# Two MLPs behind a recurrent attention: 512 tokens at a time, transposed results, and other costs in the loop that orders the work

## The chip, the cores and the metric

The kernel runs on one core of one Trainium2 chip. The metric is the device time of one execution in microseconds; the median of 3 runs counts. The engines are TensorE (PE), VectorE (DVE), ScalarE (ACT), GpSimd (POOL) and SyncE (SP), which issues most of the DMAs.

## The reference

A linear recurrence with complex decay per head (4 batches, 8 heads, 768 tokens, head size 48), then two MLPs over the 3072 tokens of 384 features:

```
a_re_n, a_im_n = a * min(|a|, 0.999) / (|a| + 1e-6)
for t in range(S):
    S_re, S_im = ar*S_re - ai*S_im + k[t] v[t]^T, ar*S_im + ai*S_re
    y[t] = q[t] @ S_re
x = y as (3072, 384)
x = relu(x @ w_in)**2 @ w_out                       # 384 -> 2048 -> 384
xn = x / sqrt(mean(x*x) + 1e-6) * rms_g
out = (silu(xn @ w_gate) * (xn @ w_val)) @ w_out2   # 384 -> 1536 -> 384
```

## The kernel before

The work is cut into 24 **units** of 128 tokens of one batch. Attention makes them two by two: a `chain` on VectorE and ScalarE normalizes the decay and multiplies it up along the tokens (`norm`, `step`, `plevel`), and for each unit PE does transposes (`dtr`, tile dps), scores (`score`, tile sps), results (`yy`, tile yps) and a state update (`state`, tile ups). `fix` moves slices of the result by six small DMAs, and `split_x` splits it into two parts for exact products in a fast float type (tile xs). With the last xs of a group its MLP can begin.

The **first MLP** takes two units at a time (`GROUPS`, L38; 256 tokens). For each of its 16 blocks f of 128 hidden features, `mlp_h` (L799) does nine matmuls with 256 columns into PSUM tile h, ScalarE makes relu and two squares of it (r, gs, h), VectorE a difference (gs), and `mlp_x` (L824) adds the block to the results x by six matmuls, with a part of gs as the stationary operand and 384 columns of weights as the moving one: a result has tokens in its partitions. `store_x` (L837) copies it out, and it goes to a DRAM tile xnd.

The **second MLP** takes three units at a time (`G2`, L938; 384 tokens). `load_x` (L941) fetches them from xnd, `rms` (L949) sums the squares of each token along its row on ScalarE, `turn` (L971) transposes them on PE (tile t), and for each of 12 blocks `mlp_g`, `mlp_v` and `mlp_o` (L998 to L1031) do nine matmuls of 384 columns each. 34 tiles of weights come as 64-bit floats; `convert` (L742) turns each into two parts with passes over ScalarE and VectorE. 18 of them belong to the second MLP, and 16 of these are loaded into the places of the first MLP's tiles as that MLP lets go of them.

The order of all this is made at build time. Each piece of work is a generator that yields an `Op` with its engine, a cost in us, buffers that it takes and gives back, and a priority; `Plan.run` (L98) holds a clock for each engine, and takes again and again the operation that can start first, by priority among those that can start at the same time. `ready` (L83) says when one can start: at the end of what it needs, plus `SYNC` and `PE_END` if that was on another engine. The instructions are issued in that order on each engine; the costs decide nothing else.

```
SYNC, PE_END, LAND = 0.13, 0.1, 2.2
LATE = {"pe": 2.0}
def dve(n): return 0.075 + 0.00104 * n
def act(n): return 0.1 + 0.00083 * n
```

Of the kernel before, what the change touches and what calls it, by code (L numbers as in the profile page):

```python
# [44 lines left out]
def dve2(n):  # L45

    return 0.11 + 0.00116 * n


def act(n):  # L50
    return 0.1 + 0.00083 * n
# [10 lines left out]
class Plan:  # L62
# [20 lines left out]
    def ready(self, j):  # L83

        t, op = j[4], j[3]
        for n in (*j[5], *op.need):
            end, eng = self.t[n]
            t = max(t, end if eng == op.eng else end + SYNC + PE_END * (eng == "pe"))
        for r in op.acq:
            k = self.taken[r] - self.counts[r]  # L90
            if k >= 0:
                if k >= len(self.back[r]):
                    return None
                end, eng = self.back[r][k]
                t = max(t, end if eng == op.eng else end + SYNC + PE_END * (eng == "pe"))
        return t

    def run(self):  # L98
        live = list(self.jobs)
        while live:  # L100
# [14 lines left out]
            for c in best.values():  # L115
                s0 = min(x[0] for x in c)
                now = [x for x in c if x[0] <= s0 + 0.02]
                old = [x for x in now if x[4] <= s0]
# [24 lines left out]
            elif j[3].free:  # L143
                j[4] = max(j[4], s)
            else:
                j[4] = end if j[3].eng == op.eng else end + SYNC + PE_END * (op.eng == "pe")


class Attention:
# [101 lines left out]
    def sumsq(self, m, s, ab, view=lambda t: t, **more):  # L251
# [5 lines left out]
        yield Op("dve", dve2(768))  # L257
# [4 lines left out]
    def norm(self, p):  # L262
# [15 lines left out]
        yield Op("dve", dve2(768))  # L278
        nc.vector.tensor_tensor(out=m, in0=m, in1=r, op=ALU.mult)
        yield Op("dve", dve2(768))  # L280
# [3 lines left out]
        yield Op("dve", dve2(768))  # L284
        nc.vector.scalar_tensor_tensor(out=m, in0=y, scalar=-2.0 / 0.999, in1=r, op0=ALU.max, op1=ALU.mult)
        d = m.rearrange("p (u j d) -> p j u d", u=2, j=8)
        for c, x in enumerate(self.raw.pop(p)):
            yield Op("dve", dve2(768), rel=["raw"] + ["tmp"] * c)
# [5 lines left out]
    def step(self, p, j):  # L294
# [3 lines left out]
        yield Op("dve", dve2(384))  # L298
# [5 lines left out]
        yield Op("dve", dve2(96))  # L304
        nc.vector.tensor_tensor(out=v[:, 0], in0=T[:, 0, 0], in1=T[:, 1, 1], op=ALU.subtract)
        yield Op("dve", dve2(96))
# [16 lines left out]
    def plevel(self, l):  # L323
# [5 lines left out]
        for t, c in ((X, 0), (Y, 1)):  # L329
# [6 lines left out]
            else:  # L336
                for e in range(2):
                    yield Op("dve", 0.2)
# [5 lines left out]
            yield Op("dve", 0.27)  # L344
            nc.vector.tensor_tensor(out=o, in0=i0, in1=i1, op=ALU.mult)
        yield Op("dve", 0.24)
        nc.vector.tensor_tensor(out=V[:, 0, :, s:], in0=X[:, 0], in1=Y[:, 1], op=ALU.subtract)
        yield Op("dve", 0.24, done=("TP", self.at) if l == 3 else None)
        nc.vector.tensor_tensor(out=V[:, 1, :, s:], in0=X[:, 1], in1=Y[:, 0], op=ALU.add)

    def chain(self, p):
# [23 lines left out]
        for n, (o, i0, i1) in enumerate(((x, a[1], f[1]), (y, a[0], f[1]), (a[0], a[0], f[0]), (a[1], a[1], f[0]))):  # L375
            yield Op("dve", dve2(768), rel=["tb"] if n == 3 else [])
            nc.vector.tensor_tensor(out=o, in0=i0, in1=i1, op=ALU.mult)
        yield Op("dve", dve2(768))
        nc.vector.tensor_tensor(out=a[0], in0=a[0], in1=x, op=ALU.subtract)
        yield Op("dve", dve2(768), rel=["tmp", "tmp"], done=("P", p))  # L380
# [19 lines left out]
    def inv(self, p):  # L400
# [13 lines left out]
        yield Op("dve", dve2(768), need=[("kin", p)])  # L414
        k = self.kin[p].rearrange("p u j d -> p (u j d)")
        nc.vector.tensor_tensor(out=m, in0=m, in1=z, op=ALU.mult)
        yield Op("dve", dve2(768))
        nc.vector.tensor_tensor(out=k, in0=k, in1=z, op=ALU.mult)
        yield Op("dve", dve2(768), rel=["tmp", "tmp"], done=("inv", p))
        nc.vector.scalar_tensor_tensor(out=k, in0=m, scalar=2.0, in1=k, op0=ALU.subtract, op1=ALU.mult)  # L420

    def prod(self, u, which):
        p, i = u // 2, u % 2
        o, t = (self.QP, self.qin[p]) if which == "q" else (self.KP[i], self.kin[p])
        for c in range(2):
            rel = [which + "in"] if (i and c) else []
            yield Op("dve", dve(384), acq=[] if c else [which + "P"], rel=rel, done=(which + "P", u) if c else None)
# [133 lines left out]
def general_path(tc, q, k, v, a_re, a_im, w, ident, gcol, out):  # L561
# [3 lines left out]
    with ExitStack() as ctx:  # L565
# [63 lines left out]
        with ExitStack() as c2:  # L629
# [33 lines left out]
            with tc.For_i(0, NT // 128, 1) as it:  # L663
# [22 lines left out]
                acc = ps.tile([128, DM], F32, tag="gacc", name="g_acc2")  # L686
                for f in range(F2):
# [5 lines left out]
                    nc.tensor.matmul(acc, lhsT=g, rhs=words(T_OUT2 + f // 2, f % 2), start=(f == 0), stop=(f == F2 - 1))  # L693
                o = sb.tile([128, DM], F32, tag="go", name="g_o")
                nc.vector.tensor_copy(o, acc)
                nc.sync.dma_start(out[bass.ds(it * 128, 128), :], o)
# [3 lines left out]
def kernel_body(ctx: ExitStack, tc, q, k, v, vt, a_re, a_im, w, rms_g, out):  # L700
# [8 lines left out]
    xnd = dram.tile([NT, DM], F32, name="xnd")  # L709
# [4 lines left out]
    psh = p1.enter_context(tc.tile_pool(name="psh", bufs=3, space=PSUM))  # L714
# [9 lines left out]
        sY=2, pe=4, xt=1, xs=2, h=3, xg=1, r=2, gs=3, x1=2, cr=2, cr2=4, xr=2, gv=3, ys=2, og=1, t=2, uu=2, us=3, ot=3,  # L724
# [17 lines left out]
    def convert(n, on_pe):  # L742

        cr, bufs = ("cr", 2) if on_pe else ("cr2", 4)
# [28 lines left out]
    def do_y(u, g, i):  # L773
        def xt():
            if i == 0:
                n = len(GROUPS[g]) * CH
                xt_t[g] = sb.tile([128, 4, n], F32, tag="xt", name="xt", bufs=1)
                xs_t[g] = sb.tile([128, 2, KT, n], F32R, tag="xs", name="xs", bufs=2)
            return xt_t[g][:, :, i * CH:(i + 1) * CH]

        if i == 0:
            yield Op("none", 0, acq=["xt", "xs"])
        yield from att.yy(u, xt)

    def fix(u, g, i):
        xt, sl = xt_t[g], slice(i * CH, (i + 1) * CH)
# [5 lines left out]
    def split_x(u, g, i):  # L792
        sl = slice(i * CH, (i + 1) * CH)
        xs = xs_t[g]
        yield from split(
            xs[:, 0, :, sl], xs[:, 1, :, sl], xt_t[g][:, 0:KT, sl], DM, rel=["xt"] if i else [], done=("xs", u)
        )

    def mlp_h(g, f):  # L799
        n = len(GROUPS[g]) * CH  # L800
        yield Op("pe", 1.06, acq=["h"], rel=["xs"] if f == F1 - 1 else [], done=("h", g, f), p=MLP_PE)
# [10 lines left out]
        yield Op("act", act(256), acq=["r"])  # L812
        r = sb.tile([128, n], F32, tag="r", name="r", bufs=2)
        nc.scalar.activation(out=r, in_=hp, func=AF.Relu)  # L814
        yield Op("act", act(256), acq=["gs"])
        gs = sb.tile([128, 2, n], F32R, tag="gs", name="gs", bufs=3)
        nc.scalar.activation(out=gs[:, 0], in_=r, func=AF.Square)  # L817
        yield Op("act", act(256), rel=["r"])
        nc.scalar.activation(out=hp, in_=r, func=AF.Square)  # L819
        yield Op("dve", dve(256), rel=["h"], done=("gs", g, f))  # L820
# [3 lines left out]
    def mlp_x(g, f):  # L824
        nb = len(GROUPS[g])
        yield Op("pe", 1.06, acq=[] if f else ["xg"], rel=["gs"], done=("x", g, f), p=MLP_PE)
        if f == 0:
            x_ps[g] = [psx.tile([128, DM], F32, tag=f"x{i}", name=f"x{i}") for i in range(nb)]
        gs = g_t.pop((g, f))
        for i in range(nb):  # L830
# [6 lines left out]
    def store_x(g, i, u):  # L837
        if i == 0:
# [289 lines left out]
```

## Time and profile before

| | |
|---|---|
| runs (us) | 1145.86, 1147.71, 1148.03 |
| median | 1147.71 us |
| profiled execution, its own time from first to last instruction (the span) | 1147.8 us |
| PE busy | 1084.5 us (94%) |
| VectorE busy | 720.2 us (63%) |
| ScalarE busy | 628.3 us (55%) |
| GpSimd busy | 100.6 us (9%) |

The profile is one execution. A share over the whole span mixes three stages: a start in which weights are converted while the first units are made, a long middle in which attention and the first MLP run together, and the second MLP alone. What a change is worth is read stage by stage. Matmuls are pipelined and their ends are modelled, so the distance from one start to the next tells PE's pace better than its busy time.

### The profile page before, as it was taken

The page shows a single profiled execution, that of the slowest core. Times are in us where ns is not written, and L with a number is a line of the kernel's source. Part 1 is how long each engine was busy: PE and PEld are TensorE (multiplying, and loading weights), DVE is VectorE, ACT ScalarE, POOL GpSimd, SP SyncE. Part 2 cuts the span into 40 slices and gives each one's busy share as a digit, 9 for nine tenths or more (in the row PEclk, how much of TensorE's full clock was granted, in tenths as well). Part 3 has the DMA queues.
Part 4 walks back from the last instruction along what each step waited for, and adds up shares of the span by engine and source line. Part 5 has one row for each costly group of instructions (what it writes and reads, how often), then busy time and mean ns, then how long its engine had stood idle before and what let it go on. Part 6 is the DMA issues. An engine that isn't in the chain of part 4 may idle for free.

```text
span 1147.8 us, 20154 instructions
## 1 busy us (share of the span) xinstructions
PE 1084.5 (94%) x7876; PEld 1039.6 (91%) x7876; DVE 720.2 (63%) x1468; ACT 628.3 (55%) x1387; POOL 100.6 (9%) x90
## 2 busy tenths in 40 slices
PE   1679889999999999999999999999999999999997
PEld 0468679999999999999999988999999999999997
DVE  5999999998989988998622579632323232222221
ACT  3878866668577766665655899432323232222221
POOL 0011123022121221220000000000000000000000
PEclk9799999999999999999999999999999999999999
DMA  8733141423514423331001780010101000000000
GB/s 276 302 87 103 33 127 47 121 55 107 143 40 121 113 68 102 87 88 38 23 11 40 253 331 2 9 33 10 33 11 32 11 32 11 12 11 11 13 9 24
DMA packets 79063, 85.41 MB, mean 74 GB/s; under 512 B 47728, under 2 KB 74608, under 8 KB 78960
## 3 DMA queue, kind: packets, MB, share of 16 engines
q1 hardware_dynamic: 78824, 83.85, 23.8%
q8 instruction: 64, 1.05, 0.4%
q14 instruction: 39, 0.32, 0.1%
q10 hardware_dynamic: 136, 0.20, 0.1%
HBM read 64.23 MB, written 18.61 MB: 72 GB/s over the span
## 4 chain that ended last, share of the span: by engine, by line
PE 83%; DVE 6%; ACT 5%; DMA 3%; issue 1%; SPq 1%; DVEq 0%; ACTq 0%
PE h L807 17%; PE x L832 17%; PE v L992 12%; PE o L1028 12%; PE g L992 12%; PE sps L467 3%; PE dps L454 3%; DMA ws<-in_w 3%; PE yps L484 2%; PE ups L502 2%; PE yps L488 2%; ACT ws L535 1%; DVE ws L537 1%; DVE cr L541 1%; ACT cr L533 1%
## 5 line engine op out<-in xcount | busy, mean ns | idle before, releaser
L807 PE MATMUL h<-xs,w 128*128 128x256 f32 x1728 | 242.2, 285 | 3.0 <-ACT w L761 1.8
L832 PE MATMUL x<-w,gs 128*128 128x384 f32 x1152 | 241.3, 344 | 2.3 <-ACT gs L817 1.3
L807 PEld LDWEIGHTS h<-xs,w 128*128 128x128 f32 x1728 | 224.8, 189 | 7.0 <-ACT w L761 2.4
L832 PEld LDWEIGHTS x<-w,gs 128*128 128x128 f32 x1152 | 194.1, 190 | 6.8 <-DVE gs L821 2.2
L1014 DVE TENSOR_TENSOR uu<-t,v 128x384 f32<-128x384 f32 x96 | 53.1, 554 | 195.8 <-PE v L992 194.5
L1028 PE MATMUL o<-w,us 128*128 128x384 f32 x864 | 166.9, 336 | 2.9 <-ACT us L729 2.5
L992 PE MATMUL g<-ys,w 128*128 128x384 f32 x864 | 167.0, 337 | 1.3 <-DVE w L731 0.5
L992 PE MATMUL v<-ys,w 128*128 128x384 f32 x864 | 167.4, 338 | 0.0
L1028 PEld LDWEIGHTS o<-w,us 128*128 128x128 f32 x864 | 151.0, 188 | 5.1 <-ACT us L729 3.1
L992 PEld LDWEIGHTS g<-ys,w 128*128 128x128 f32 x864 | 151.7, 188 | 2.7 <-DVE w L731 1.4
L992 PEld LDWEIGHTS v<-ys,w 128*128 128x128 f32 x864 | 150.3, 188 | 0.1
L814 ACT ACTIVATE r<-h 128x256 f32<-128x256 f32 x192 | 72.9, 380 | 122.9 <-PE h L807 122.4
L1005 ACT ACTIVATE t<-g 128x384 f32<-128x384 f32 x96 | 47.3, 493 | 159.9 <-PE g L992 159.8
L729 ACT CAST us<-uu 128x384 fp32r<-128x384 f32 x96 | 49.2, 513 | 131.2 <-DVE uu L1014 131.2
L821 DVE TENSOR_TENSOR gs<-h,gs 128x256 fp32r<-128x256 f32 x192 | 80.4, 419 | 58.8 <-ACT h L819 57.9
L731 DVE TENSOR_TENSOR us<-uu,us 128x384 fp32r<-128x384 f32 x96 | 53.6, 558 | 50.2 <-ACT us L729 50.2
L817 ACT ACTIVATE gs<-r 128x256 fp32r<-128x256 f32 x192 | 80.3, 418 | 8.7 <-PE x L832 2.7
L512 POOL TENSOR_TENSOR Y<-W,pe 48x384 f32<-48x384 f32 x40 | 52.1, 1302 | 320.3 <-DVE W L508 174.6
L819 ACT ACTIVATE h<-r 128x256 f32<-128x256 f32 x192 | 71.2, 371 | 0.0
L467 PE MATMUL sps<-dq,dk 112*128 112x128 f32 x384 | 52.6, 282 | 4.3 <-ACT dq L456 1.8
L467 PEld LDWEIGHTS sps<-dq,dk 112*128 112x128 f32 x384 | 49.3, 197 | 6.2 <-ACT dq L456 2.7
L300 DVE TENSOR_TENSOR XY<-A 128x384 f32<-128x384 f32 x84 | 49.0, 583 | 2.2
(123 smaller groups left out, 1338.7 us busy)
## 6 DMA issues: line engine op xcount, KB each, us to landing
ws<-in_w SPq DMA_DIRECT2D x34, 768.0 KB
kb<-KP SPq DMA_DIRECT2D x20, 448.0 KB
kt<-kb SPq DMA_DIRECT2D x20, 448.0 KB
raw<-in_a_re SPq DMA_DIRECT2D x24, 192.0 KB
raw<-in_a_im SPq DMA_DIRECT2D x24, 192.0 KB
kin<-in_k SPq DMA_DIRECT2D x24, 192.0 KB
qin<-in_q SPq DMA_DIRECT2D x24, 192.0 KB
V<-in_vt SPq DMA_DIRECT2D x24, 192.0 KB
```

The lines of the kernel that those rows point to most:

```text
L467: nc.tensor.matmul(P[:, i], lhsT=K[:, h, :], rhs=Q[:, h, :], start=True, stop=True)
L512: nc.gpsimd.tensor_tensor(out=Y[dst:dst + D], in0=W[src:src + D], in1=im[src:src + D].to_broadcast([D, H, D]), op=ALU.mult)
L731: nc.vector.tensor_tensor(out=lo, in0=src, in1=hi.bitcast(F32), op=ALU.subtract)
L807: nc.tensor.matmul(hp, lhsT=part(f, 0, a)[:, kk * 128:(kk + 1) * 128], rhs=xs[:, bb, kk, :], start=(i == 0), stop=(i == 8),)
L814: nc.scalar.activation(out=r, in_=hp, func=AF.Relu)
L817: nc.scalar.activation(out=gs[:, 0], in_=r, func=AF.Square)
L819: nc.scalar.activation(out=hp, in_=r, func=AF.Square)
L821: nc.vector.tensor_tensor(out=gs[:, 1], in0=hp, in1=gs[:, 0].bitcast(F32), op=ALU.subtract)
L832: nc.tensor.matmul(x_ps[g][i], lhsT=gs[:, a, i * CH:(i + 1) * CH], rhs=part(f, 1, bb), start=(f == 0 and n == 0), stop=(f == F1 - 1 and n ...
L992: nc.tensor.matmul(P, lhsT=part(T_GATE + f, half, a)[:, kk * 128:(kk + 1) * 128], rhs=ys[:, bb, kk, :], start=(i == 0), stop=(i == 8),)
L1014: nc.vector.tensor_tensor(out=uu, in0=t_t.pop((g, f)), in1=P, op=ALU.mult)
L1028: nc.tensor.matmul(o_ps[g][i], lhsT=us[:, a, i * CH:(i + 1) * CH], rhs=part(T_OUT2 + f // 2, f % 2, bb), start=(f == 0 and n == 0), stop=( ...
```

## The change

- The first MLP takes its first four units two by two as before, then four units (512 tokens) at a time; the second MLP takes four units at a time.
- `mlp_x` and `mlp_o` swap their operands: 128 columns of weights are the stationary operand, and gs (us) with all tokens of the group the moving one. Results have features in their partitions; xnd and the output are transposed, and the host turns the output back.
- The sum of squares now runs along partitions: two matmuls with a matrix of ones (tile rsum) replace the transposes t, and the normalization works on whole tiles of 128 x 512 and 128 x 1536.
- Buffers: h 3 to 2, gs 3 to 2, one xr and one ys for each of two pools.
- The loop that orders the work has other costs, adds a time after an operation for the next one that needs it also on the same engine (not on PE), marks independent neighbours as `free` (they may start with the one before), and may wait up to 0.3 us for an operation of very high priority.

The diff, cut to its core:

```diff
-SYNC, PE_END, LAND = 0.13, 0.1, 2.2
+LAND = 2.2
+AFTER = {"pe": 0.2, "dve": 0.115, "act": 0.095, "pool": 0.12}
+URGENT, NEAR = -250, 0.3
 LATE = {"pe": 2.0}
-GROUPS = [[2 * i, 2 * i + 1] for i in range(12)]
+GROUPS = [[0, 1], [2, 3]] + [list(range(u, u + 4)) for u in range(4, 24, 4)]
+def mm(k, n):
+    return k * (0.006 + 0.0004375 * n)
 def dve(n):
-    return 0.075 + 0.00104 * n
+    return 0.067 + n / 960
 def act(n):
-    return 0.1 + 0.00083 * n
+    return 0.097 + n / 1200
+def after(of, to):
+    return 0.0 if of == to == "pe" else AFTER.get(of, 0.0)
...
-                t = max(t, end if eng == op.eng else end + SYNC + PE_END * (eng == "pe"))
+                t = max(t, end + after(eng, op.eng))
...
+                now += [x for x in c if s0 + 0.02 < x[0] <= s0 + NEAR and x[1] <= URGENT]
-                old = [x for x in now if x[4] <= s0]
+                old = [x for x in now if x[4] <= max(s0, x[0])]
...
+    def turned_out(ps, w, src, first, last):
+        for e in range(KT):
             for n, (a, bb) in enumerate(PASS):
                 nc.tensor.matmul(
-                    x_ps[g][i], lhsT=gs[:, a, i * CH:(i + 1) * CH], rhs=part(f, 1, bb),
-                    start=(f == 0 and n == 0), stop=(f == F1 - 1 and n == 2),
+                    ps[e], lhsT=w(bb)[:, e * 128:(e + 1) * 128], rhs=src[:, a, :],
+                    start=(first and n == 0), stop=(last and n == 2),
                 )
...
+            need = [("xs", u) for u in us] + [("w", f, 0), ("w", f if g == 0 else F1 - 1, 1)]
...
-    G2 = [[3 * i, 3 * i + 1, 3 * i + 2] for i in range(8)]
+    G2 = [[4 * i + j for j in range(4)] for i in range(6)]
...
+        yield Op("pe", mm(2, N2), acq=["gv"])
+        P = P2["psg"].tile([128, N2], F32, tag="gv", name="rsum")
+        for i in range(2):
+            nc.tensor.matmul(P, lhsT=ones, rhs=hl[:, i], start=(i == 0), stop=(i == 1))
```

The change makes another order of nearly all instructions. Three places of it follow.

The first place is PE between the second pair of units (group 1) and the next group of the first MLP. Before, with x_1674 and x_1675 the results of group 1 and x_2281, x_2282 those of group 2:

```order
L807 MATMUL h<-xs,w 128x256 x9
L454 MATMUL dps<-ident,KP_90 112x128 x4
L832 MATMUL x_1674<-w,gs 128x384 x3
L832 MATMUL x_1675<-w,gs 128x384 x3
L807 MATMUL h<-xs,w 128x256 x18
L832 MATMUL x_2281<-w,gs 128x384 x3
L832 MATMUL x_2282<-w,gs 128x384 x3
```

Now, where the first h of 512 columns stands (yps of the eighth unit ahead of it, dps and sps belong to the ninth):

```order
L491 MATMUL yps<-st,V_90 64x128 x2
L495 MATMUL yps<-dq,St_102 48x128 x2
L461 MATMUL dps<-ident,QP 112x128 x8
L461 MATMUL dps<-ident,KP_91 112x128 x8
L826 MATMUL h<-xs,w 128x512 x9
L474 MATMUL sps<-dq,dk 128x128 x4
```

Before, h of the next pair stands among the last blocks of the pair before it; now the last x of group 1 stands 56 rows ahead of the first h of the quad, and between them are only attention's instructions, those of the seventh and the eighth unit.

The second place is VectorE in the attention chain, some way before the eighth unit is ready (A is the decay, XY a product of two of its steps, kin the keys). Before:

```order
L821 TENSOR_TENSOR gs<-h,gs 128x256
L300 TENSOR_TENSOR XY<-A_86 128x384
L305 TENSOR_TENSOR A_86<-XY 128x96
L307 TENSOR_TENSOR A_86<-XY 128x96
L300 TENSOR_TENSOR XY<-A_86 128x384
L821 TENSOR_TENSOR gs<-h,gs 128x256
```

Now:

```order
L425 TENSOR_TENSOR kin<-kin,z 128x768
L840 TENSOR_TENSOR gs<-h,gs 128x256
L427 SCALAR_TENSOR_TENSOR kin<-m,kin 128x768
L312 TENSOR_TENSOR A_87<-XY 128x96
L435 TENSOR_TENSOR KP_91<-A_88,kin 128x8x48 x2
L314 TENSOR_TENSOR A_87<-XY 128x96
```

Before, an A reads the XY just before it and the next XY the A just before it; now a row of other work stands between an instruction and the one that reads it.

The third place is ScalarE around the change from the first to the second MLP. Before, around the first silu (t) of the second MLP (cr, ws and w are the passes of a conversion):

```order
L729 CAST w<-cr 128x768
L551 ACT_TABLE_LOAD
L551 ACTIVATE rs_y<-ss 128x3
L533 ACTIVATE cr<-ws 128x768
L535 ACTIVATE ws<-ws 128x768
L533 ACTIVATE cr<-ws 128x768
L729 CAST us<-uu 128x384
L1005 ACT_TABLE_LOAD
L1005 ACTIVATE t<-g 128x384
```

Now, one step f of the last quad of the first MLP:

```order
L540 ACTIVATE cr<-ws 128x768
L833 ACTIVATE r<-h 128x512
L745 CAST w<-cr 128x768
L542 ACTIVATE ws<-ws 128x768
L836 ACTIVATE gs<-r 128x512
L838 ACTIVATE h<-r 128x512
```

Before, the first silu has six of the 18 conversions' last pass (w) ahead of it; now each step of the last quad holds one conversion, and 16 stand ahead of the first silu.

## Rows read from the trace of the kernel before

**Rows 1.** The page: span, busy us with share and instructions by engine, PE's 40 slices.
```profile
span 1147.8 us, 20154 instructions
...
PE 1084.5 (94%) x7876; PEld 1039.6 (91%) x7876; DVE 720.2 (63%) x1468; ACT 628.3 (55%) x1387; POOL 100.6 (9%) x90
...
PE   1679889999999999999999999999999999999997
```

**Rows 2.** Timeline, PE, second MLP: start us, us, engine line op names shapes xcount.
```profile
900.43 1.73 PE L992 MATMUL g<-ys,w 128*128 128x384 f32 x9
...
905.12 1.72 PE L992 MATMUL g<-ys,w 128*128 128x384 f32 x9
...
911.37 0.49 PE L978 MATMUL t<-ident,xr 128*128 128x128 f32 x3
911.62 0.59 PE L992 MATMUL v<-ys,w 128*128 128x384 f32 x2
```

**Rows 3.** Timeline, PE, first MLP behind the last attention block.
```profile
620.76 1.34 PE L807 MATMUL h<-xs,w 128*128 128x256 f32 x9
621.94 1.21 PE L832 MATMUL x<-w,gs 128*128 128x384 f32 x6
622.99 1.23 PE L807 MATMUL h<-xs,w 128*128 128x256 f32 x9
624.06 1.21 PE L832 MATMUL x<-w,gs 128*128 128x384 f32 x6
```

**Rows 4.** Windows: stretch, us, PE PEld DVE ACT POOL busy (x), PEclk, DMA share, GB/s.
```profile
164.10:202.20 38.10, 38.02 (x364) 36.92 (x365) 35.23 (x80) 26.28 (x65) 9.98 (x8) 1.00 0.29 78
202.20:260.40 58.20, 57.88 (x512) 56.04 (x511) 54.72 (x122) 39.03 (x97) 11.04 (x8) 1.00 0.35 95
260.40:305.00 44.60, 44.60 (x415) 43.23 (x413) 40.65 (x87) 30.26 (x75) 9.65 (x8) 1.00 0.37 100
305.00:351.40 46.40, 46.40 (x428) 44.76 (x427) 41.46 (x88) 31.92 (x79) 9.52 (x8) 1.00 0.34 93
```

**Rows 5.** Timeline, DVE, around the xs of the 12th unit.
```profile
350.00 0.56 DVE L300 TENSOR_TENSOR XY<-A 128x384 f32<-128x384 f32 x1
350.48 0.42 DVE L821 TENSOR_TENSOR gs<-h,gs 128x256 fp32r<-128x256 f32 x1
350.81 0.55 DVE L731 TENSOR_TENSOR xs<-xt,xs 128x384 fp32r<-128x384 f32 x1
```

**Rows 6.** Timeline, PE, first h of the sixth pair.
```profile
356.34 1.23 PE L807 MATMUL h<-xs,w 128*128 128x256 f32 x9
```

**Rows 7.** Lines by form, DVE: xcount | busy us, mean ns | idle before us.
```profile
L377 DVE TENSOR_TENSOR x<-A,back 128x768 f32<-128x768 f32 x24 | 22.0, 946 | 2.3 <-PE back L365 2.2
```

**Rows 8.** Timeline, DVE, a step of the attention chain.
```profile
300.63 0.56 DVE L300 TENSOR_TENSOR XY<-A 128x384 f32<-128x384 f32 x1
301.23 0.26 DVE L305 TENSOR_TENSOR A<-XY 128x96 f32<-128x96 f32 x1
```

**Rows 9.** Timeline, PE, the longest wait after the first MLP.
```profile
684.72 1.55 PE L1028 MATMUL o<-w,us 128*128 128x384 f32 x6 [1.51 <-ACT us L729]
```

**Rows 10.** Lines by form, ScalarE (ACT).
```profile
L814 ACT ACTIVATE r<-h 128x256 f32<-128x256 f32 x192 | 72.9, 380 | 122.9 <-PE h L807 122.4
...
L1005 ACT ACTIVATE t<-g 128x384 f32<-128x384 f32 x96 | 47.3, 493 | 159.9 <-PE g L992 159.8
L535 ACT ACTIVATE ws<-ws 128x768 int32<-128x768 uint8 x34 | 31.3, 920 | 0.0
...
L729 ACT CAST w<-cr 128x768 fp32r<-128x768 f32 x18 | 15.1, 841 | 2.8 <-DVE cr L541 2.8
```

**Rows 11.** Timeline, all engines, the end.
```profile
1140.16 0.48 ACT L1040 COPY ot<-o 128x384 f32<-128x384 f32 x1 [0.57 <-PE o L1028]
1140.67 1.21 ACTq L1043 DMA_DIRECT2D out<-ot  x1
```

**Rows 12.** Windows, the second MLP, columns as in rows 4.
```profile
800.00:900.00 100.00, 100.00 (x582) 99.82 (x581) 31.11 (x65) 33.60 (x69) 0.00 (x0) 1.00 0.08 25
```

More of the change, by code (lines that the diff above doesn't have):

```diff
@@ L145, in run @@
             else:
[L146 removed]
+                j[4] = end + after(op.eng, j[3].eng)
 class Attention:
@@ new lines, in turned_out, with mlp_x, store_x @@
+                    start=(first and n == 0), stop=(last and n == 2),
+                )
+    def mlp_x(g, f):
+        n = len(GROUPS[g]) * CH
+        yield Op("pe", mm(9, n), acq=[] if f else ["xg"], rel=["gs"], done=("x", g, f), p=MLP_PE)
+        if f == 0:
+            x_ps[g] = [psx.tile([128, n], F32, tag=f"x{e}", name=f"x{e}") for e in range(KT)]
+        turned_out(x_ps[g], lambda bb: part(f, 1, bb), g_t.pop((g, f)), f == 0, f == F1 - 1)
+    def store_x(g, e):
+        n = len(GROUPS[g]) * CH
+        yield Op("dve" if e == 1 else "act", dve(n), acq=["r"], done=("xc", g, e))
+        x = sb.tile([128, n], F32, tag="r", name="x1", bufs=2)
+        if e == 1:
+            nc.vector.tensor_copy(x, x_ps[g][e])
+        else:
+            nc.scalar.copy(out=x, in_=x_ps[g][e])
+        yield Op("sp", 0.65, rel=["r"], mb=0.27, done=("xnd", g, e))
+        nc.sync.dma_start(xnd[e * 128:(e + 1) * 128, GROUPS[g][0] * CH:GROUPS[g][0] * CH + n], x)
@@ L1023, in mlp_o @@
         if f == 0:
-            o_ps[g] = [P2["pso"].tile([128, DM], F32, tag=f"o{i}", name=f"o{i}") for i in range(nb)]
-        us = u_t.pop((g, f))
-        for i in range(nb):
-            for n, (a, bb) in enumerate(PASS):
-                nc.tensor.matmul(
-                    o_ps[g][i], lhsT=us[:, a, i * CH:(i + 1) * CH], rhs=part(T_OUT2 + f // 2, f % 2, bb),
-                    start=(f == 0 and n == 0), stop=(f == F2 - 1 and n == 2),
-                )
-    def store(g, i):
-        b, c = att.bc(G2[g][i])
-        yield Op("dve" if i == 1 else "act", dve(DM), acq=["ot"], done=("oc", g, i))
-        t = P2["sb"].tile([128, DM], F32, tag="ot", name="ot", bufs=3)
-        if i == 1:
-            nc.vector.tensor_copy(t, o_ps[g][i])
-        else:
-            nc.scalar.copy(out=t, in_=o_ps[g][i])
-        end = (g, i) == (len(G2) - 1, 2)
-        yield Op("act" if end else "sp", 0.65, mb=0.2, rel=["ot"])
-        (nc.scalar if end else nc.sync).dma_start(
-            out[b * S_LEN + c * CH:b * S_LEN + (c + 1) * CH, :].rearrange("(p j) e -> j p e", j=8), t
-        )
+            o_ps[g] = [P2["pso"].tile([128, N2], F32, tag=f"o{e}", name=f"o{e}") for e in range(KT)]
@@ new lines, in mlp_o, with store @@
+        turned_out(o_ps[g], lambda bb: part(T_OUT2 + f // 2, f % 2, bb), u_t.pop((g, f)), f == 0, f == F2 - 1)
+    def store(g, e):
+        yield Op("dve" if e == 1 else "act", dve(N2), acq=["ot"], done=("oc", g, e))
+        t = P2["late"].tile([128, N2], F32, tag="ot", name="ot", bufs=3)
+        if e == 1:
+            nc.vector.tensor_copy(t, o_ps[g][e])
+        else:
+            nc.scalar.copy(out=t, in_=o_ps[g][e])
+        end = (g, e) == (len(G2) - 1, 2)
+        yield Op("act" if end else "sp", 0.65, mb=0.27, rel=["ot"])
+        dst = out[e * 128:(e + 1) * 128].rearrange("e (b c t) -> e b c t", b=B, c=NC)[:, :, g, :]
+        (nc.scalar if end else nc.sync).dma_start(dst, t.rearrange("e (b t) -> e b t", b=B))
@@ L1065, in kernel_body @@
             plan.job(s + LAG2 + 0.2, mlp_o(g, f), ["open3", ("us", g, f), ("w", T_OUT2 + f // 2)] + before)
[L1066 to L1068 removed]
+        for e in range(KT):
+            plan.job(t0 + F2, store(g, e), [("o", g, F2 - 1)])
+        plan.job(t0, join([("oc", g, e) for e in range(KT)], ["og"]))
     order = []
@@ L1081, in kernel_body @@
         nc.scalar.mul(minus, ident, -1.0)
+        nc.scalar.activation(out=ones, in_=ident, func=AF.Copy, scale=0.0, bias=1.0)
         nc.sync.dma_start(gcol, rms_g.rearrange("(k p) -> p k", p=128))
```

277 lines of the change are left out of this document (133 added, 144 removed).

## The prediction, made before the changed kernel ran

> **What bounds the kernel now.** I read the page first [rows 1]: TensorE (PE) is busy for 1084.5 of 1147.8 us, and the digits of the 40 slices stand at 9 from the seventh on. The ends of matmuls are modelled, so I then read their spacing in the timeline. In the second MLP [rows 2] g starts at 900.43 and the next g at 905.12: 27 matmuls of 384 columns in 4.69 us, 173.7 ns each, back to back. In the first MLP [rows 3] nine h matmuls of 256 columns take 1.07 us (119 ns each) behind an MLP block, and six x matmuls of 384 take 1.05; the h that follows an attention block (yps) takes 1.18, so a switch from attention back to an MLP costs about 0.1. Wherever PE has work it runs at its rate; the end is PE's work plus the time in which it had none.
>
> The second view is the table of windows, whose bounds I set where a group's last xs is ready: the 4th, 6th, 8th, 10th and 12th unit of 128 tokens [rows 4]. PE is full in all four, but VectorE (DVE) is busy for 35.23 + 54.72 + 40.65 + 41.46 = 172.1 of 187.3 us. So while attention runs there are two bounds, and units arrive at VectorE's pace. The 12th xs ends at 351.36 [rows 5], and h of the sixth pair starts at 356.34 [rows 6].
>
> **The change, part by part.** I work out when h of the first quad that needs the 12th unit's successors can start, that is the quad of units 8 to 11, and add what is then left. The sum is made on the profiled span of 1147.8 us, 0.1 above the median of the runs.
>
> *The pair that comes later.* A group of four units can start only when its fourth is ready. Before, the pairs of units 4, 5 and 6, 7 ran while the next were made; now, by the order, PE has after group 1 only attention until the eighth unit is ready (first place above). When units 8 to 11 are ready, PE has therefore done four pairs' worth where before it had done five (the sixth started at 356.34). A pair is 16 x (1.07 + 1.05) = 33.9 us [rows 3]. PE's idle time in between cannot be won back, since PE is the bound in all that follows.
>
> *When the 12th unit is ready.* Both orders put almost the same number of VectorE instructions before it, 653 and 650. Counted by kind: gs of 256 goes from 78 to 32, with 16 of 512 beside them. A gs is followed after 0.33 us (350.48 to 350.81), a 384-wide product after 0.48 (350.00 to 350.48) [rows 5], so 512 is 0.62 [estimate]: 25.7 against 20.5 us, -5.2. Copies of x: -0.6. In their place the new order holds some 27 more of the attention chain, five of 768 (0.946) [rows 7] and the others small, like the 0.26 at 301.23: +9.2 with their overlap taken off. Neighbours where one reads what the one before writes go from 176 to 136; such a pair costs 0.12 (300.63 to 301.23 is 0.60 against the 0.48) [rows 8]: -4.8. Together -1.4. Of VectorE's 15.2 us idle in rows 4 I take 3 as gone, because PE stands ready for attention in the empty stretch; the bounds are 0 and 11. So the 12th xs ends at 351.4 - 1.4 - 3 = 347.0, and h starts 1.4 later, at **348.4** (bounds 338 and 352). The lower bound is PE's: the eighth unit has 443 instructions before it where it had 480, and 48 dependent neighbours fewer, about 18 us in all, so it comes at 242.4; from there 16 x 4.12 for the quad and 28 for attention with its switches (before: 356.3 - 260.4 = 96 less two pairs of 33.9) give 242.4 + 1.4 + 94 = 338.
>
> *What is left from there.* Before, 1147.8 - 356.3 = 791.5 us.
> - One pair more: +33.9. Two x blocks of the group before, still to do at 356.3 and done by now: -2.1.
> - Wider matmuls. From 256 to 384 columns the spacing grows by 55 ns; the same step again gives 229 ns for 512 [estimate]. A quad is 16 x 2 x 9 x 0.229 = 66.0 against 67.8 for two pairs: four quads, -7.4. The second MLP: 96 x 4.69 = 450.2 against 72 x 27 x 0.229 = 445.2, -5.0. Bounds of the one unknown: 227.0 (128 more columns at 2.4 GHz, 53.3 ns) and 231.6 (in proportion to 384), on 3,096 such matmuls from there on and 288 before: -7 and +9.
> - The transposes: 24 blocks of 0.25 us (911.37 to 911.62) [rows 2] go, six rsum of two 512-column matmuls (0.46) come: -3.3. With 18 switches fewer: -1.8.
> - Switches between attention and MLP from there on, counted in the order: 77 become 61, -1.6.
> - From the first to the second MLP. PE waited for us behind weight conversions on ScalarE, 1.51 us the longest [rows 9]; five such waits stand in the timeline, 4.0 us. In the order (third place above) six of the 18 tiles were converted when ScalarE came to its first silu; now it is 16. I take -3.0; bounds -4 and +4. The cost is that each step of the last quad now holds three 512-wide activations and one conversion. By the rows 256 takes 0.380 and 384 takes 0.493 [rows 10], so 512 about 0.61; 3 x 0.61 and a conversion's three passes of 0.92, the same again and 0.84 would be 4.5 us against PE's 4.12, but activations that follow each other overlap by nearly 0.1, six times, which brings it to 3.9.
> - The tail: last copy at 1140.16, last store at 1140.67 [rows 11]. The copy is a third wider and the store goes out in rows of 128 tokens instead of 384 features: +0.7, bounds 0 and +1.5.
> - Nothing: SyncE issues fewer transfers (stores of x 24 to 21, loads of it 24 to 6, outputs 24 to 18), the larger rms work on ScalarE and VectorE lies beside a second MLP that leaves both about 67% idle [rows 12] (cover gone: about 5 us for a group), and two buffers of h and gs instead of three have 2 us of slack a step (a rival, below).
>
> That is 791.5 + 33.9 - 2.1 - 7.4 - 5.0 - 3.3 - 1.8 - 1.6 - 3.0 + 0.7 = 801.9, and **348.4 + 801.9 = 1150.3 us**. The wider matmuls and the smoother order give back nearly all of the late pair, and no more.
>
> The Trainium skill (TensorE: Matmul & The Clock Gate, Back-to-back issue gap) gives the spacing of an isolated warm matmul as its columns at 2.4 GHz plus 2.5 ns, 162.5 ns at 384 and 215.8 at 512. With 215.8 for 229 the sum would be some 45 us lower; but the trace has 173.7 where the rule has 162.5, in a stream with a weight load before each matmul, so the measurement decides. Of the rule only the price of a further column remains open, and that is the second rival below.
>
> **The rivals.** *VectorE stops waiting* (faster). The order now prices dependent steps and so fills the gaps; if its idle time in rows 4 falls from 15.2 to about 7, PE decides and the quad starts at 340: 1142. For it: the new order puts other work between dependent steps (second place above). Against it: the four stretches are already 92% busy, and the empty stretch has fewer gs to fill gaps with. It decides below some 8 us of idle between the 4th and the 12th unit. *A matmul has a fixed part* (faster): if further columns cost just 2.4 GHz, 512 takes 227.0 ns, and 3,384 of them give 1143.5. Two sizes cannot exclude it, but 119 and 173.7 lie on a line with 55, not 53.3. *Two buffers* (slower): ScalarE cannot square step f+2 before x of step f has freed gs; from there two squares, the subtraction and their hand-overs take 2.0 us, and PE wants the h buffer 4.1 us later. One 768-wide activation and one 768-wide product in the way use that up; 0.1 us in each of 80 steps is 8 us: 1158. *The order's own times are short* (slower): it prices a 768-wide product at 0.867 us where the row has 0.946 [rows 7]. If that 9% is real on the 172 us of rows 4, PE waits in its fixed order where the plan thinks all is ready, and some 10 us of it come on top: 1160. Against it: an independent neighbour follows a 384-wide product after 0.48, close to the 0.467 of the plan.
>
> **How the numbers follow.** The forecast gets 0.43, with 1146 to 1155 of its own from the bounds of the start of the quad and of the tail; VectorE stops waiting 0.27; the fixed part 0.08; the two slower ones 0.22 together. Over 0.2% (about what a measurement here can tell) means below 1145.4 or above 1150.0. The forecast lies on the upper edge: about 0.20 of its chance is the same, 0.23 slower. So faster 0.28 (0.22 + 0.06), same 0.27, slower 0.45. The range of 8 in 10 reaches from the two faster cases to the two slower ones: 1140 to 1161.
>
> **What would show it.** Right: in the windows of the new profile PE is clearly below full between about 200 and 243 us; VectorE stays above 90% until the 12th xs near 347; h of the fourth group starts at 346 to 350; h of 512 steps in 2.06; the waits of o for us are gone; PE is full from 350 to the end. Wrong: the quad starts before 342 or after 353, the spacing at 512 is not 229 within 1, or PE shows waits for gs or h inside the quads.

## The result, and the profile after

The changed kernel takes **1164.45 us** (median of 4 runs) against 1147.87 of the kernel before: 1.0145 times the time, 95% interval 1.0117 to 1.0172. It is 16.6 us slower, where 1150.3 was forecast; even the upper end of the range, 1161, was too low. The profiled execution spans 1163.3 us. Its page (columns as in rows 1):

```profile
span 1163.3 us, 16402 instructions
...
PE 1078.7 (93%) x6304; PEld 887.9 (76%) x6304; DVE 715.7 (62%) x1317; ACT 582.9 (50%) x1040; POOL 106.7 (9%) x90
...
PE   1678988969999999999998999999999999999997
...
PEclk9789999979999999999999899999999999999999
```

PE is 5.8 us less busy than in [rows 1], in a span 15.5 us longer. Behind the start two places stand out, and at both the granted clock dips: the ninth slice of 29 us, where PE has a stretch with little to do, and the 22nd and 23rd. The table of windows (columns as in rows 4), cut where groups start:

```profile
200.00:245.00 45.00, 34.75 (x357) 32.20 (x356) 41.51 (x85) 27.55 (x63) 13.50 (x8) 0.90 0.36 97
245.00:350.00 105.00, 102.31 (x775) 85.04 (x774) 97.10 (x211) 61.98 (x123) 23.47 (x18) 0.98 0.39 102
...
537.00:624.00 87.00, 87.00 (x528) 72.89 (x527) 28.73 (x45) 42.01 (x76) 0.00 (x0) 1.00 0.07 20
624.00:697.00 73.00, 67.65 (x276) 54.01 (x275) 53.95 (x72) 60.29 (x90) 0.00 (x0) 0.93 0.53 182
```

The empty stretch before 245 us is there as forecast, and VectorE (DVE) is still 92% busy from 200 to 350. The timeline around the 12th xs, VectorE first and then PE, answers to [rows 5, 6]:

```profile
348.25 0.55 DVE L747 TENSOR_TENSOR xs<-xt,xs 128x384 fp32r<-128x384 f32 x1
...
349.16 2.11 PE L826 MATMUL h<-xs,w 128*128 128x512 f32 x8
```

The 12th xs ends at 348.8 (forecast 347.0) and the quad starts at 349.2 (forecast 348.4). So the first half of the sum held; what is left from there took 1163.3 - 349.2 = 814.1 us where I had 801.9. The last row of the windows tells where: of the 73 us of the last quad of the first MLP, PE is busy for 67.65, at a mean clock of 0.93. Here are PE in it, VectorE and ScalarE (x of nine at 628.38 is the last of the quad before):

```profile
628.38 2.30 PE L846 MATMUL x<-gs,w 128*128 128x512 f32 x9
630.52 4.48 PE L826 MATMUL h<-xs,w 128*128 128x512 f32 x18
635.46 0.49 PE L991 MATMUL rsum<-rs_h,ones 128*128 128x512 f32 x1 [0.45 <-ACT rs_h L745]
636.18 0.50 PE L991 MATMUL rsum<-rs_h,ones 128*128 128x512 f32 x1 [0.23 <-DVE rs_h L747]
636.52 0.85 PE L846 MATMUL x<-gs,w 128*128 128x512 f32 x3
640.11 6.39 PE L846 MATMUL x<-gs,w 128*128 128x512 f32 x15 [2.74 <-DVE x L863]
648.44 3.46 PE L826 MATMUL h<-xs,w 128*128 128x512 f32 x9 [1.93 <-DVE gs L840]
```
```profile
637.03 0.96 DVE L544 SCALAR_TENSOR_TENSOR ws<-ws 128x768 int32<-128x768 int32 x1 [0.90 <-ACT ws L542]
637.90 0.68 DVE L993 TENSOR_SCALAR rs_s<-rsum 128x512 f32<-128x512 f32 x1
638.50 0.95 DVE L548 SCALAR_TENSOR_TENSOR cr<-cr,ws 128x768 int32<-128x768 int32 x1
639.37 0.68 DVE L863 COPY x<-x 128x512 f32<-128x512 f32 x1
```
```profile
629.41 0.59 ACT L865 COPY x<-x 128x512 f32<-128x512 f32 x1 [0.37 <-PE x L846]
...
642.18 1.24 ACT L833 ACTIVATE r<-h 128x512 f32<-128x512 f32 x2 [0.90 <-DMA xnd<-x]
```

The first of the three copies of the previous quad's results follows at once (629.41). The second (L863) runs at 639.37, though PE finished that quad at 630.5. PE cannot go on with the new x before it (the results fill all three PSUM banks), and waits 2.74 us; the waits of rsum and h bring it to 5.35. Behind them the clock is at its lower level, 1.2 GHz (half). ScalarE's last row shows the buffer at issue: r of the new quad waits until a store of x (xnd) has landed. The windows of that piece:

```profile
638.00:640.00 2.00, 0.00 (x0) 0.00 (x0) 2.00 (x4) 1.38 (x3) 0.00 (x0) 0.77 0.00 0
640.00:646.00 6.00, 5.89 (x14) 4.63 (x15) 5.96 (x10) 4.04 (x7) 0.00 (x0) 0.51 0.51 179
646.00:648.00 2.00, 0.50 (x3) 0.07 (x1) 2.00 (x4) 1.29 (x2) 0.00 (x0) 1.00 0.62 157
648.00:650.00 2.00, 1.56 (x6) 1.24 (x7) 1.88 (x2) 1.50 (x3) 0.00 (x0) 0.83 0.83 335
650.00:652.00 2.00, 2.00 (x6) 1.61 (x5) 0.87 (x2) 0.00 (x1) 0.00 (x0) 0.50 0.41 52
652.00:654.00 2.00, 2.00 (x8) 1.59 (x8) 0.00 (x0) 2.00 (x3) 0.00 (x0) 0.81 0.94 354
```

PE's busy time times the missing share of the clock is 5.89 x 0.49 + 1.56 x 0.17 + 2.00 x 0.50 + 2.00 x 0.19 = 4.5 us of lost work. Idle 5.35 and 4.5 of clock are most of what the forecast lacked.

### The profile page after: what moved, and what is told of

The parts are those of the page before. It is cut to its first block, busy times and chain, and to the rows that moved or that the text cites. A ratio compares the mean times of both kernels' runs of the same rounds, so it can differ in the third digit from the quotient of the medians.

```text
span 1163.3 us, 16402 instructions
## 1 busy us (share of the span) xinstructions
PE 1078.7 (93%) x6304; PEld 887.9 (76%) x6304; DVE 715.7 (62%) x1317; ACT 582.9 (50%) x1040; POOL 106.7 (9%) x90
## 4 chain that ended last, share of the span: by engine, by line
PE 78%; DVE 15%; ACT 2%; issue 2%; DMA 1%; SPq 0%; DVEq 0%; ACTq 0%
PE x L846 14%; PE h L826 14%; PE o L846 13%; PE g L1015 13%; PE v L1015 13%; PE sps L474 3%; PE dps L461 2%; PE yps L491 1%; PE ups L509 1%; DVE XY L307 1%; PE yps L495 1%; DVE ws L544 1%; DVE cr L548 1%; DVE gs L840 1%; DVE KP L435 1%
## 5 line engine op out<-in xcount | busy, mean ns | idle before, releaser
L826 PE MATMUL h<-xs,w 128*128 128x512 f32 (+1 forms) x1008 | 227.8, 372 | 10.7 <-DVE gs L840 9.4
L846 PE MATMUL x<-gs,w 128*128 128x512 f32 (+1 forms) x1008 | 227.7, 371 | 8.1 <-DVE gs L840 4.5
L846 PEld LDWEIGHTS x<-gs,w 128*128 128x128 f32 x1008 | 173.7, 194 | 39.0 <-DVE gs L840 5.7
L846 PE MATMUL o<-us,w 128*128 128x512 f32 x648 | 162.0, 395 | 0.0
L1015 PE MATMUL g<-ys,w 128*128 128x512 f32 x648 | 161.1, 393 | 0.0
L1015 PE MATMUL v<-ys,w 128*128 128x512 f32 x648 | 160.8, 392 | 0.0
L846 PEld LDWEIGHTS o<-us,w 128*128 128x128 f32 x648 | 121.7, 188 | 28.7
L836 ACT ACTIVATE gs<-r 128x512 fp32r<-128x512 f32 (+1 forms) x112 | 63.8, 569 | 73.8 <-PE x L846 57.1
L833 ACT ACTIVATE r<-h 128x512 f32<-128x512 f32 (+1 forms) x112 | 59.9, 535 | 71.0 <-PE h L826 66.3
L840 DVE TENSOR_TENSOR gs<-h,gs 128x512 fp32r<-128x512 f32 (+1 forms) x112 | 68.1, 608 | 43.6 <-ACT h L838 43.5
```

Source lines behind the costliest of these rows:

```text
L826: nc.tensor.matmul(hp, lhsT=part(f, 0, a)[:, kk * 128:(kk + 1) * 128], rhs=xs[:, bb, kk, :], start=(i == 0), stop=(i == 8),)
L840: nc.vector.tensor_tensor(out=gs[:, 1], in0=hp, in1=gs[:, 0].bitcast(F32), op=ALU.subtract)
L846: nc.tensor.matmul(ps[e], lhsT=w(bb)[:, e * 128:(e + 1) * 128], rhs=src[:, a, :], start=(first and n == 0), stop=(last and n == 2),)
L1015: nc.tensor.matmul(P, lhsT=part(T_GATE + f, half, a)[:, kk * 128:(kk + 1) * 128], rhs=ys[:, bb, kk, :], start=(i == 0), stop=(i == 8),)
```

## The experiments

### The width and the order apart

Two kernels take the change apart. One has the changed code with the costs and rules of the order as before:

```diff
-LAND = 2.2
-AFTER = {"pe": 0.2, "dve": 0.115, "act": 0.095, "pool": 0.12}
-URGENT, NEAR = -250, 0.3
+SYNC, PE_END, LAND = 0.13, 0.1, 2.2
...
-            yield Op("dve", dve(768), rel=["raw"] + ["tmp"] * c, free=c == 1)
+            yield Op("dve", dve2(768), rel=["raw"] + ["tmp"] * c)
```

> The changed kernel with the costs and rules of the order as before. Theory W: still slow, 1162 to 1170 us, and TensorE's empty stretch ahead of the first group of four units is still there. Theory P: 1150 to 1156 us.

Measured: 1158.58 us (1.0089 times the time before, 1.0072 to 1.0106). The other is the kernel before with the new order and nothing else:

> The kernel before with the new costs, the new rule for what may start, and the marks for independent neighbours, and nothing else. Theory W: the order is not what costs; the 12th xs ends 1 to 4 us earlier than 351.4 and the time is 1143 to 1148 us. Theory P: slower than 1152 us.

Measured: 1167.8 us (1.0179, 1.0154 to 1.0205). Neither theory's number came for the first, and theory W fell on the second: the order alone costs 20 us in narrow groups, and in the changed kernel 6. Two kernels with other groups were to show what the quads cost:

```diff
-GROUPS = [[0, 1], [2, 3]] + [list(range(u, u + 4)) for u in range(4, 24, 4)]
+GROUPS = [[u, u + 1] for u in range(0, 24, 2)]
```

> Theory W (the fourth unit): what costs is that a group of four units starts one pair later, while TensorE has nothing else. Pairs in the first MLP then take TensorE's idle time up to 350 us from 71 us back to about 54 (that of the kernel before), against some 6 us for narrower matmuls: about 1153 us, and the stretch without MLP work near 224 to 245 us is gone. Theory P (the order): the new costs and the tighter buffers are what costs, and stay: 1160 us or more, and TensorE's idle time up to 350 us stays above 65.

Measured: 1179.62 us (1.0275, 1.0257 to 1.0294): slower still, so that in this code quads are better than pairs throughout. And with `[[0, 1], [2, 3], [4, 5], [6, 7]]` ahead of four quads:

> Theory W: the eighth unit's wait goes, but at the 12th xs TensorE has again done only four pairs' worth; the idle time moves to about 290 to 349 us and the total stays: 1162 to 1167 us. Rival theory E: the one empty stretch before 245 us, with the low granted clock behind it, is the whole loss (10 us of idle and about 4 of clock): 1150 us.

Measured: 1156.61 us (1.0069, 1.0052 to 1.0086), between the two. Its 245 to 349 us do not hold the idle time that theory W moved there (windows of that kernel):

```profile
200.00:245.00 45.00, 42.97 (x429) 40.23 (x428) 41.85 (x88) 31.22 (x75) 7.81 (x8) 1.00 0.36 97
245.00:290.00 45.00, 43.20 (x421) 41.13 (x420) 43.57 (x103) 28.88 (x73) 7.61 (x6) 1.00 0.33 92
290.00:349.00 59.00, 56.22 (x591) 52.75 (x590) 52.56 (x121) 37.06 (x87) 13.21 (x12) 1.00 0.47 123
```

PE lacks 2.0 + 1.8 + 2.8 = 6.6 us here; in the changed kernel it lacks 12.9 from 200 to 350 us. What the change is worth without its order stands in the kernel with the old order: PE is 1074.8 us busy in its span of 1156.5, 9.7 less than before, but its idle time up to the last matmul is 73.1 us where it was 55.6. Groups, swapped operands and second MLP together save 9.7 us of work and pay 17.5 of idle time for it.

### What in the order costs: prices or rules

> The kernel before with the lower prices of VectorE and ScalarE operations, and nothing else new. Theory M (the prices leave no room for what happens on VectorE, above all the some 30 us that its instructions take longer beside GpSimd): the order runs ahead of the chip, PE waits in its fixed order, the last xs comes 8 us or more after 628.5, and the time is 1157 us or more. Theory R (the new rules put filling work ahead of what PE waits for): 1145 to 1151 us.

Measured: 1178.21 us (1.0257, 1.023 to 1.0284).

> The kernel before with the time after an operation, the marks for independent neighbours and the short wait for an urgent one, but with the prices of before. Theory M: 1143 to 1151 us, and no wait of x for the copy of x longer than 1 us. Theory R: 1157 us or more, with those waits at the start of groups as in the order-only kernel (2.5 to 4 us each).

Measured: 1152.55 us (1.0044, 1.0027 to 1.006), 1.5 above theory M's range. Here is what PE waited for between 345 and 560 us, first with the prices alone; with the rules alone that view is empty.

```profile
engine line waited for: us in total, times, longest us
PE x L832 <- DVE x L841: 10.1, 4, 3.1
```

It is again the copy of results out of PSUM. One such place in the order-only kernel, VectorE and then GpSimd and PE:

```profile
421.34 1.69 DVE L292 SCALAR_TENSOR_TENSOR m<-A 128x768 f32<-128x768 f32 x1 [0.58 <-ACT A L290]
423.06 2.98 DVE L296 TENSOR_TENSOR A<-raw,m 128x768 f32<-128x768 f32 x2
425.96 0.54 DVE L848 COPY x<-x 128x384 f32<-128x384 f32 x1
```
```profile
422.29 2.93 POOL L519 TENSOR_TENSOR Y<-W,pe 48x384 f32<-48x384 f32 x2
```
```profile
426.65 1.28 PE L839 MATMUL x<-w,gs 128*128 128x384 f32 x6 [2.59 <-DVE x L848]
```

Products of 768 that take 0.95 us elsewhere take 1.5 to 1.7 beside GpSimd; the copy stands behind them, and PE behind the copy. The order's clock allows 0.867 for each. The old price of such a product was 0.11 + 0.00116 x 768 = 1.0, which left some room. With the prices alone a dependent step on the same engine is also free, where the rows have 0.12 us for it; the new rules price that, and both together are 10 us faster than the prices alone (1167.8 against 1178.2).

How far the plan ran ahead can be read off: the loop that makes the order holds a clock, and its time for the last xs (computed at build, no time of the chip) stands here beside the trace.

```
last xs, us             planned  measured   lag    time
before                    617.2     628.5   11.3   1147.9
new prices alone          607.7     652.2   44.5   1178.2
new rules alone           625.4     627.1    1.7   1152.6
order alone (both)        611.8     642.2   30.4   1167.8
order alone, no GpSimd    618.4     628.1    9.7   1152.3
changed kernel            597.9     624.0   26.1   1164.5
changed, no GpSimd        604.8     614.4    9.6   1156.6
changed, old prices       630.1     638.0    7.9   1168.7
```

The last row is this one, the changed kernel with its new rules and the prices of before:

> The changed kernel (512 tokens, its rules) with the prices of before on VectorE and ScalarE. Theory M: some 8 us come back, 1154 to 1159 us. Theory R: 1162 us or more.

Measured: 1168.65 us (1.0183, 1.0163 to 1.0203): theory R's number came, not theory M's. In wide groups the new rules with the old prices cost 10 us (1158.6 with neither), and the new prices give 4 back. The lag is small, but the plan itself is long: a dependent step now pays the room in the old price and the new time after it too. An honest plan is not yet a good one. That this is the reason is argued from the prices, and was not tried apart.

### Without GpSimd

The test of theory M takes GpSimd's four products per unit to VectorE, which gets 80 more operations for it:

```diff
-            yield Op("pool", 1.1, need=[("pe", u)] + ([("St", u - 1)] if u else []))
-            nc.gpsimd.tensor_tensor(
+            yield Op("dve", dve(384), need=[("pe", u)] + ([("St", u - 1)] if u else []))
+            nc.vector.tensor_tensor(
...
```

> The order-only kernel (the kernel before with all new costs and rules) with the state's four products on VectorE instead of GpSimd: 80 more operations of 384 on VectorE, some 37 us, and no GpSimd beside it. Theory M (the new prices are right for VectorE alone, and fail where GpSimd slows it): VectorE's instructions show their plain durations, the last xs comes within 12 us of its planned 618, the waits of x for the copy of x are gone, and the time is 1146 to 1156 us. If the prices fail for another reason: 1160 us or more.

Measured: 1152.31 us (1.0033, 1.002 to 1.0046), 15.5 less than with GpSimd, though VectorE has some 37 us more to do; its busy time grows by only 8.5 (711.8 to 720.3). The lag falls to 9.7, and no wait for the copy is left. A shorter way through the state is not the reason: with GpSimd, neither PE nor VectorE waits for any of its four products. All 24 executions of the product L296, in the order-only kernel and then without GpSimd (duration ns min/median/max):

```profile
L296 DVE TENSOR_TENSOR A<-raw,m x24: 940/948/1582, 15.1 to 529.5; 128x768 f32<-128x768 f32 x24
```
```profile
L296 DVE TENSOR_TENSOR A<-raw,m x24: 948/952/958, 15.2 to 506.5; 128x768 f32<-128x768 f32 x24
```

Whether that also holds in wide groups:

> The changed kernel with the state's four products on VectorE instead of GpSimd, all else the same. Theory M (in the changed kernel too the plan runs ahead of the chip because GpSimd slows VectorE): the last xs's lag behind the plan falls from 26 us to 12 or less, and 4 to 10 us come off: 1154 to 1160 us. If only the groups of four and the copies are left: the 37 us more of VectorE's own work make it no faster, 1163 us or more.

Measured: 1156.63 us (1.0083, 1.0057 to 1.0109; runs from 1152.9 to 1159.9): 7.8 off the changed kernel, with the lag at 9.6 (in the fastest of the four). So GpSimd's part of theory M is shown for both widths; that in wide groups the short prices cost time is not, since there the old ones did not help.

### The copies, and the second MLP alone

> The changed kernel with buffers of their own for the copies of x of all groups but the last (the places of the conversion tiles, which are idle by then), where the change let them share r's two. Theory S (the last quad's 8 us of lost time, 5.4 of idle and the low clock behind it, come from copies that wait for r until a store has landed): the copies follow the last x within 3 us, PE has no wait over 1 us between 620 and 660 us, the granted clock stays at 1.0 there, and the time is 1153 to 1157 us. If the conversions and the normalization are what fills VectorE there, whatever the copies do: 1161 us or more.

```diff
-        yield Op("dve" if e == 1 else "act", dve(n), acq=["r"], done=("xc", g, e))
-        x = sb.tile([128, n], F32, tag="r", name="x1", bufs=2)
+        yield Op("dve" if e == 1 else "act", dve(n), acq=["cr" if g < last else "r"], done=("xc", g, e))
+        x = (asb.tile([128, n], F32, tag="cr", name="x1", bufs=2) if g < last else sb.tile(...))
...
-    plan.job(T2 - F1, open2(), ["flag"])
+    plan.job(T2 - F1, open2(), ["flag"] + [("xnd", last - 1, e) for e in range(KT)])
```

Measured: 1158.39 us (1.0076, 1.0051 to 1.0102), 6.1 off. The window of 620 to 660 us, in the changed kernel and then in this one:

```profile
620.00:660.00 40.00, 34.65 (x131) 26.65 (x130) 23.86 (x37) 26.14 (x39) 0.00 (x0) 0.87 0.48 162
```
```profile
620.00:660.00 40.00, 40.00 (x177) 32.44 (x176) 17.63 (x28) 26.55 (x44) 0.00 (x0) 1.00 0.47 180
```

The idle time and the low clock are gone together, and h of the last quad runs from 624.4 to 689.9, 65.5 us where it was 73.1. All signs of theory S came but the time, which is 1.4 above its range; the other order starts the quad of units 8 to 11 at 352.9, 3.7 later. The run moves a second thing, though: the last line of its edit makes the second MLP's first conversions and its normalization wait for these stores too, so that they no longer stand ahead of the copies on VectorE. Which of the two holds the second copy back in the changed kernel, the clock of the loop tells (computed at build): there the last x ends at 604.8, the first copy's store lands at 617.55, and the second copy starts at 617.58, when r comes free. The loop takes that store to land 11.9 us after its copy, behind earlier loads; on the chip these stores take 2.2 us (median) from issue to landing. In the kernel with the old order, with the same shared buffers, only the third copy waits for a store, 1.6 us. So the sharing costs by the place that the new order gives the copies. With four pairs ahead:

> The same with four pairs ahead of the quads. If the two effects are separate, both come off: 1157 less 4 to 8, that is 1148 to 1153 us. If the pairs had only moved the same loss elsewhere: 1155 us or more.

Measured: 1151.75 us (1.0028, 1.0015 to 1.0041), as expected. With GpSimd left out as well, it did not add up:

> Four pairs ahead of the quads, own buffers for the copies, and no GpSimd. If all three losses are separate: 1141 to 1147 us. If the 37 us more on VectorE take it back: 1150 us or more.

Measured: 1158.09 us (1.0081, 1.0062 to 1.01). In this order PE waits twice for an xs ahead of h, 7.7 us, the longer time 5.0; each gain came through an order of its own, and they do not sum.

What is left of the change with everything else as before is one term of the forecast. First the swapped operands in both MLPs, in pairs, with the old order:

> The changed kernel with the costs and rules of before and groups of two units in the first MLP (three buffers of gs): only the swapped operands and 512 tokens in the second MLP are left of the change. If the order alone is at fault (theory M or R), the second MLP's 5 us and the transposes' 3 us come out, less up to 4 us at its start: 1138 to 1145 us. If the swapped operands or the wider normalization cost something themselves: 1148 us or more.

Measured: 1167.48 us (1.0177, 1.0148 to 1.0207). The swapped x takes 120 ns a matmul at 256 columns, nine times, where six of 384 took 175; that is 1.08 against 1.05 us and no more than 6 us in all. PE waits for gs before h ten times (7.9 us), as it does in the pairs with the new order (19 times, 18.7 us); before, it had three buffers of h, now two. That these buffers are the reason was not tried: the three banks of x leave no room for a third h. Together this is 14 of the 20 us; the rest stays open. Then the second MLP alone:

> The kernel before in attention, first MLP and order, with the second MLP alone at 512 tokens (its transposes kept), and with us and all ys but the first placed in memory that the first MLP leaves. Theory W2 (the wide second MLP is a gain of 5.7 us by itself): 1139 to 1144 us. Spacing: if the two values that the changed kernel shows, 226.7 ns for h, x and every second group's g and v, and 232.6 for the rest, hang on where the moving operand lies, then o and the g and v of groups 1 to 5 all show 226.7 here, and another 6 us come off: 1133 to 1139 us. If not, o stays at 232 to 233.

Measured: **1137.85 us** (0.9893, 0.9868 to 0.9918), faster than both kernels. The spacing tells the two parts of the edit apart, the width and the place of the buffers. The timeline of PE in the changed kernel, at the end of the first group of the second MLP, in the second and in the third, and then in this kernel:

```profile
770.92 2.21 PE L1015 MATMUL g<-ys,w 128*128 128x512 f32 x9
772.96 2.20 PE L1015 MATMUL v<-ys,w 128*128 128x512 f32 x9
775.00 2.21 PE L846 MATMUL o<-us,w 128*128 128x512 f32 x9
...
787.83 2.26 PE L846 MATMUL o<-us,w 128*128 128x512 f32 x9
789.93 2.21 PE L1015 MATMUL g<-ys,w 128*128 128x512 f32 x9
791.97 2.20 PE L1015 MATMUL v<-ys,w 128*128 128x512 f32 x9
794.01 2.27 PE L846 MATMUL o<-us,w 128*128 128x512 f32 x9
...
887.99 2.26 PE L846 MATMUL o<-us,w 128*128 128x512 f32 x9
890.09 2.26 PE L1015 MATMUL g<-ys,w 128*128 128x512 f32 x9
892.19 2.26 PE L1015 MATMUL v<-ys,w 128*128 128x512 f32 x9
894.29 2.26 PE L846 MATMUL o<-us,w 128*128 128x512 f32 x9
```
```profile
916.89 2.20 PE L1001 MATMUL g<-ys,w 128*128 128x512 f32 x9
918.93 2.20 PE L1001 MATMUL v<-ys,w 128*128 128x512 f32 x9
920.97 2.20 PE L1032 MATMUL o<-us,w 128*128 128x512 f32 x9
```

Nine matmuls step by 2.04 us (226.7 ns each) or by 2.10 (233.3). In most blocks of the changed kernel o takes 2.10, and g and v do so in every second group, the ones whose ys lies with us in the memory that attention left. But the moving operand alone does not decide. Two of the 18 tiles of weights, those of the last g and v of a group and of its last two o, lie in the memory that attention left too, and there the values change places: in the first group the last g and v and the o behind them (770.92 to 777.05) take 2.04 to 2.05, and in the second group the last g and v (845.61 to 849.81) take 2.10. So the step is 2.04 where weights and moving operand lie in the same of the two memories, and 2.10 where they lie in different ones. In this kernel, from its second group on, only the blocks with those two tiles are the slow ones.

## Why the prediction was wrong

**What held.** The late pair, the bound by VectorE, the time of the 12th xs (348.8 against 347.0) and the start of the quad (349.2 against 348.4). That these two came so near is in part luck: up to the 12th xs VectorE's busy time is 5.1 us less than before (310.6 against 315.6), not the 1.4 of my count, and its idle time 2.5 more where I had 3 less. So did the tail (8.3 us after the last matmul, 7.7 before: +0.6, forecast +0.7) and the second MLP: its g, v and o take 449.0 us, 455.3 before without their waits, -6.3 against -5.0 and part of the switches' -1.8.

**The step that failed** is "From the first to the second MLP ... I take -3.0; bounds -4 and +4". The five waits of the kernel before are gone, as I said; only three of them, 2.9 us, were of o for us [rows 9], the other two of g. In their place the last quad holds 5.35 us of idle time and 4.5 of low clock, 9.9 against the 4.0 before: +5.9, outside my bounds. I had reckoned ScalarE's time per step, but put the stores of x and the normalization at "Nothing". The change lets the copies of x share r's two buffers with h, a store holds its buffer until it has landed, and the loop takes that to be late; so the second and third copy came 9 us late, behind conversions and the normalization of the second MLP's first group, and PE, VectorE and ScalarE stood in their fixed order behind them. That a stall of 2.7 us is followed by 6 us at the lower clock was in no term at all. Undoing the sharing, with the order that comes of it, gave 6.1 us back and the clock with it.

**A second step**: PE was to be full from 350 us on. It lacks 2.1 us in the quads between 349 and 537. Together with the transition's 8.9 (5.9 instead of -3.0) that is 11.0 of the 12.2 us by which the remainder was too short. The rest is not split up further. Two of my own signs of being wrong came as well: the spacing at 512, and waits for gs inside the quads (three, 2.9 us, 1.9 of it in the last quad).

**The price at 512** was 229 ns; it is 226.7 or 233.3, by whether weights and moving operand lie in the same memory, 231.0 over the second MLP. The fixed part that I gave 0.08 is there: 173.7 - 384/2.4 = 13.7 ns and 226.7 - 512/2.4 = 13.4. Its saving was eaten by the second value, which nothing before showed.

**The rivals.** "The order's own times are short" was right and worth more than its chance. Its mechanism was half right: the plan is short, but not for the 0.867 against 0.946 that I weighed. In the order-only kernel independent products of 768 do follow each other after 0.87 us (414.39, 415.26, 416.13). What the prices leave out is GpSimd, which lengthens some of VectorE's instructions to nearly twice their time. I had its row in view and let it pass. "Two buffers" was the right worry at the wrong buffer: r, not gs. "VectorE stops waiting" did not happen: between the xs of the 4th and the 12th unit (161.7 to 348.8 us) VectorE is idle for 14.6 us, 15.2 before, so that not even the 3 us that I took came; the 12th xs was earlier by less work ahead of it, all of it before the 4th unit.

So of the 16.6 us, 10.7 are there with the old order, and the new order adds 5.9; undoing its cost at the copies gave 6.1 back and leaving GpSimd out 7.8. The first quad costs: four pairs ahead of the quads save 7.8. Quads throughout do not: against pairs of the same code they are 9 us faster with the old order (1158.6 against 1167.5, the pairs with a third gs) and 15 with the new (1164.5 against 1179.6). What else makes up the 10.7 stays open.

## What to carry to other kernels

A fixed order made from times needs room in them where engines slow each other: shorter prices cost 30 us in the narrow kernel, 20 with dependent steps priced too, and leaving GpSimd out gave back 15.5 of these 20. When a buffer is shared, ask how long the order's clock thinks its longest holder keeps it (here a store until it has landed, 11.9 us against 2.2), what PE does meanwhile and what the clock does after. Test parts of a large change alone: one third of this one, the second MLP at 512 tokens with the old order and its buffers placed by the weights, was worth 10 us.

## What the runs showed of the hardware that was not expected

- Some of VectorE's instructions that read two operands from SBUF are stretched beside GpSimd, from 0.95 up to 1.77 us at 768; those with one operand in PSUM are not. All 24 of each in the changed kernel (raw and m lie in SBUF, back in PSUM):

```profile
L296 DVE TENSOR_TENSOR A<-raw,m x24: 943/950/1769, 15.4 to 501.7; 128x768 f32<-128x768 f32 x24
...
L384 DVE TENSOR_TENSOR x<-A,back x24: 936/947/955, 32.7 to 534.6; 128x768 f32<-128x768 f32 x24
```

  The Trainium skill (GPSIMD Engine Reference, Specifications) says that GpSimd's SBUF interfaces are shared with VectorE and that instructions with two SBUF inputs contend; the trace agrees on both kinds. The page gives no price; here it is up to 0.8 us for one instruction, and not beside every one of GpSimd's: in the order-only kernel a product of 768 (L288, 419.47) takes its plain 0.95 beside GpSimd's St<-W,pe (L523, 419.33 to 421.11).
- A 512-column matmul costs 226.7 ns where its weights and its moving operand lie in the same of the two memories of this kernel, and 233.3 where they lie in different ones. Which property of the places decides was not tried.
- After waits of 0.45, 0.23 and 2.74 us PE ran at half clock from before 640 until about 646, though by then it was busy for 5.89 of 6 us, and again from 650 to 652, behind the wait of 1.93.
